# A transformer block on one core: prologue without GpSimd fills and DMA spreads, and a modelled list schedule in place of fixed alternation

## Chip, cores and metric

The kernel runs on one core of one Trainium2 chip. The metric is the device time of one execution in microseconds (us), as the median over several executions. A trace shows one execution, and its span is some 2 us shorter than the reported time. Ratios: the mean time of one kernel's runs over that of the kernel before in the same rounds. So a ratio is not quite the ratio of the medians quoted beside it.

## The reference, cut to what matters

```python
# x: (1, 2048, 512) bf16; 32 heads of 16; gated layer of width 1792
def block(x, wqkv, wo, w_gate, w_up, w_down):
    n = layernorm(x)
    q, k, v = split_heads(n @ wqkv)                      # 32 heads, Dh = 16
    p = softmax(q @ k.T * Dh ** -0.5)                    # 32 x 2048 x 2048 exponentials
    h = x + merge_heads(p @ v) @ wo
    m = layernorm(h)
    return h + (sigmoid(m @ w_gate) * (m @ w_up)) @ w_down
```

The exponentials are the bulk. There are 134 million of them, that is 2048 units of 128 x 512 (4 chunks of 512 queries, 8 groups of 4 heads, 16 key tiles, 4 heads).

## The kernel before: the parts that matter

Three units make one tile of scores, so there are 683 tiles. The matmul engine (PE) writes a tile's scores into one of two PSUM buffers of three banks, ScalarE takes the exponential, and PE multiplies it by the values ("value matmuls", into `acc`). In some tiles (here called splits) ScalarE does only two units. VectorE computes the third one in seven instructions, of which the first, J, is the one that frees the bank. All other work (projections for later heads, output projection, layernorm and gated layer of the chunk before) is "background": generators that hand out matmuls two at a time into one further PSUM bank, `pm`.

The prologue fills constant rows with memsets, some of them on GpSimd:

```python
    for g in range(2):
        nc.vector.memset(QT[g][:], 0.0)
    nc.vector.memset(KT[0][:], 1.0)
    nc.gpsimd.memset(KT[1][:], 1.0)
    nc.gpsimd.memset(Vaug[:, :, :, DH:VW], 0.5)
    # ... (layernorm, transposes, first projections: see the whole kernel)
    for g in range(2, NG):                      # no input: GpSimd starts them at once
        nc.gpsimd.memset(QT[g][:], 0.0)
        nc.gpsimd.memset(KT[g][:], 1.0)
```

The main loop alternates by a fixed rule. Even tiles get up to eight value matmuls, and odd ones get four background matmuls. VectorE's work is placed by two running clocks:

```python
        if n % 2 == 0:
            av(8)
            run_bg(0)
        else:
            tokens -= run_bg(4 if tokens >= 4 else 0)     # +1.3 tokens per tile, no cap
        run_chain(clock["A"] + 600)                       # VectorE's chain, up to 0.6 us ahead
        clock["D"] = max(clock["D"], clock["A"] - 600)
```

Of the kernel before, what the change touches and what calls it, by code (L numbers as in the profile page):

```python
# [28 lines left out]
def kernel(  # L29
# [12 lines left out]
    P = 128  # L42
# [30 lines left out]
    eps4_t = const.tile([P, 1], FP32)  # L73
    sel = const.tile([P, 32], BF16)
    xnT = [const.tile([P, DC, QC], BF16, name=f"xnT{c}") for c in range(NQC)]
# [12 lines left out]
    wv_sb = prep.tile([P, DC, D], BF16)  # L88

    wqkv_v = A_wqkv.rearrange("(c p) n -> p c n", p=P)  # L90
    x_v = A_x[0].rearrange("(t p) d -> p t d", p=P)
    for i, q in enumerate((nc.sync, nc.scalar, nc.sync, nc.scalar)):
        q.dma_start(out=xb[0][:, i, :], in_=x_v[:, i, :])
    nc.sync.dma_start(out=xb[1][:], in_=x_v[:, TQ:2 * TQ, :])
    nc.scalar.dma_start(out=wk_sb[:], in_=wqkv_v[:, :, D:2 * D])
    nc.sync.dma_start(out=xb[2][:], in_=x_v[:, 2 * TQ:3 * TQ, :])
    nc.scalar.dma_start(out=wq_sb[:], in_=wqkv_v[:, :, 0:D])
    nc.sync.dma_start(out=xb[3][:], in_=x_v[:, 3 * TQ:4 * TQ, :])
    nc.sync.dma_start(out=wv_sb[:], in_=wqkv_v[:, :, 2 * D:3 * D])

    make_identity(nc, ident_bf[:])
    nc.vector.memset(eps_t[:], 1e-5)
    nc.vector.memset(eps4_t[:], 4e-5)
    nc.gpsimd.tensor_scalar(out=ident2[:], in0=ident_bf[:], scalar1=2.0, scalar2=None, op0=ALU.mult)
    nc.vector.memset(sel[:], 0.0)
    nc.vector.tensor_reduce(out=sel[:, 0:8], in_=ident_bf[:].rearrange("p (r k) -> p r k", k=DH),
                            axis=AX.X, op=ALU.max)
    for g in range(2):
        nc.vector.memset(QT[g][:], 0.0)
    nc.vector.memset(KT[0][:], 1.0)  # L110
    nc.gpsimd.memset(KT[1][:], 1.0)
    nc.gpsimd.memset(Vaug[:, :, :, DH:VW], 0.5)
    wo_v = A_wo.rearrange("(p a j d) n -> a j d p n", a=2, j=4, d=DH)


    clock = {"D": 0.0}

    def dv(ns):
        clock["D"] += ns

    def ln_stats(src, mv):
        dv(870)
        st = small.tile([P, nc.vector.BN_STATS_DIM], FP32, name="st")
        nc.vector.bn_stats(out=st[:], in_=src)
        nc.vector.bn_aggr(out=mv, in_=st[:])
# [13 lines left out]
    def spread(dst_pair, src, cols, groups=(0, 1), queues=(nc.sync,)):  # L139
        for a in groups:  # L140
            for j in range(4):
                r = (4 * a + j) * DH
                queues[j % len(queues)].dma_start(out=dst_pair[a][32 * j:32 * j + DH, cols],  # L143
                                                  in_=src[r:r + DH, :])

    def stage(ps, name):
        dv(680)
        st = work.tile([P, QC], BF16, name=name, bufs=2)
        nc.vector.tensor_copy(out=st[:], in_=ps)
        return st  # L150

    def square(src):
        dv(430)
        sq = work.tile([P, QC], BF16, name="sq", bufs=4)
        nc.vector.tensor_tensor(out=sq[:], in0=src[:], in1=src[:], op=ALU.mult)
        return sq

    def k_fin(k4, p):
        dv(300)
        nc.vector.tensor_reduce(out=kcol[p][:], in_=k4[:], axis=AX.X, op=ALU.max)  # L160
        nc.vector.tensor_scalar(out=kcol[p][:], in0=kcol[p][:], scalar1=-0.505, scalar2=None,
                                op0=ALU.mult)

    def q_shift(ps, p):
        dv(740)
        sh = work.tile([8, QC], BF16, name="sh")
        nc.vector.tensor_scalar(out=sh[:], in0=ps[0:8, :], scalar1=-0.505,
                                scalar2=kcol[p][:, 0:1], op0=ALU.mult, op1=ALU.add)
        for a in range(2):
            nc.sync.dma_start(out=QT[2 * p + a][DH:P:32, :], in_=sh[4 * a:4 * a + 4, :])  # L170
# [6 lines left out]
    def v_out(ps, t, act):  # L177
        dst = Vaug[:, t, :, 0:DH]
        src = ps.rearrange("p (h d) -> p h d", d=DH)
        if act:  # L180
            nc.scalar.copy(out=dst, in_=src)
        else:
            dv(680)
            nc.vector.tensor_copy(out=dst, in_=src)

# [9 lines left out]
    NV0 = 6  # L195
    k4 = small.tile([8, NQC], FP32, name="k4a", bufs=1)
    mvs, rstds = {}, {}
    kps, sqs0 = {}, {}

    def c_stats(c):  # L200
        mvs[c] = small.tile([P, TQ, nc.vector.BN_AGGR_DIM], FP32, name="mv")
        for i in range(TQ):
            ln_stats(xb[c][:, i, :], mvs[c][:, i, :])
        rstds[c] = small.tile([P, TQ], FP32, name="rstd")
        nc.scalar.activation(out=rstds[c][:], in_=mvs[c][:, :, 1], func=ACT.Sqrt,
                             bias=eps_t[:, 0:1])

    def c_apply(c, dve):
        nc.vector.reciprocal(out=rstds[c][:], in_=rstds[c][:])
        for i in range(TQ):  # L210
# [4 lines left out]
            pt = transpose4(bank0(), xn)  # L215
            dst = xnT[c][:, :, i * P:(i + 1) * P]
            if i in dve:
                nc.vector.tensor_copy(out=dst, in_=pt)
            else:
                nc.scalar.copy(out=dst, in_=pt)  # L220

    def c_keys(c):
        pk = bank0()
        proj8(pk, wk_sb, 0, c)
        kd = work.tile([P, QC], BF16, name="kd", bufs=2)
        nc.scalar.copy(out=kd[:], in_=pk)
        cols = slice(c * QC, (c + 1) * QC)
        if c < NQC - 1:
            spread(KT[0:2], kd, cols)
        else:  # L230
            spread(KT[0:2], kd, cols, groups=(0,), queues=(nc.sync, nc.scalar))
        kps[c] = kd

    def c_ksq(c):
        sq = square(kps[c])
        pm = bank0()
        nc.tensor.matmul(pm[0:8, :], lhsT=sel[:, 0:8], rhs=sq[:], start=True, stop=True)
        return pm

    def c_kred(c, pm):  # L240
        nc.vector.tensor_reduce(out=k4[:, c:c + 1], in_=pm[0:8, :], axis=AX.X, op=ALU.max)

    def c_v(t):
        ps = bank0()
        v_mm(ps, t)
        v_out(ps, t, True)

    c_stats(0)
    c_stats(1)
    c_apply(0, ())  # L250
    c_stats(2)
    c_keys(0)
    c_apply(1, ())
    pq = bank0()
    proj8(pq, wq_sb, 0, 0)
    qd = work.tile([P, QC], BF16, name="qd", bufs=2)
    nc.scalar.copy(out=qd[:], in_=pq)
    spread(QT[0:2], qd, slice(0, QC))
    c_stats(3)
    c_keys(1)  # L260
    c_apply(2, (0, 2))
    pm0 = c_ksq(0)
    sqq = square(qd)
    pq = bank0()
    nc.tensor.matmul(pq[0:8, :], lhsT=sel[:, 0:8], rhs=sqq[:], start=True, stop=True)
    c_apply(3, (0, 1, 3))
    c_keys(2)
    c_kred(0, pm0)
    pm1 = c_ksq(1)
    c_kred(1, pm1)  # L270
    c_v(0)
    c_keys(3)
    pm2 = c_ksq(2)
    c_kred(2, pm2)
    c_v(1)
    nc.scalar.activation(out=small.tile([P, 1], FP32, name="warm")[:], in_=eps_t[:], func=ACT.Exp)
    pm3 = c_ksq(3)
    c_kred(3, pm3)
    k_fin(k4, 0)
    q_shift(pq, 0)  # L280
    spread(KT[0:2], kps[NQC - 1], slice((NQC - 1) * QC, S), groups=(1,))
    for t in range(2, NV0):
        c_v(t)
    for a in range(2):
        for j in range(4):
            r = 32 * j + DH * a
            nc.gpsimd.dma_start(out=wo_sb[r:r + DH, :, :], in_=wo_v[a, j])
    for g in range(2, NG):
        nc.gpsimd.memset(QT[g][:], 0.0)
        nc.gpsimd.memset(KT[g][:], 1.0)  # L290
# [14 lines left out]


    EV = "ev"

    def prep_v(t):
        yield 2  # L310
        ps = pm_tile()
        v_mm(ps, t, 0, 2)
        yield 2
        v_mm(ps, t, 2, 4)
        yield EV
        v_out(ps, t, False)

    kpend = {}

    def prep_k(p):  # L320
        sqs = []
        for c in range(NQC):
            yield 2
            ps = pm_tile()
            proj8(ps, wk_sb, p, c, 0, 2)
            yield 2
            proj8(ps, wk_sb, p, c, 2, 4)
            yield EV
            kd = stage(ps, "kd")
            spread(KT[2 * p:2 * p + 2], kd, slice(c * QC, (c + 1) * QC))  # L330
            sqs.append(square(kd))
        yield 2
# [4 lines left out]
        yield EV  # L337
        dv(680)
        kr = small.tile([P, 1], FP32, name="kr")
        nc.vector.tensor_reduce(out=kr[:], in_=ps, axis=AX.X, op=ALU.max)  # L340
        kq = small.tile([8, NQC], FP32, name="k4")
        for c in range(NQC):
            nc.sync.dma_start(out=kq[:, c:c + 1], in_=kr[32 * c:32 * c + 8, :])
        kpend[p] = kq

    def prep_q(qc, p):
        yield 2
        ps = pm_tile()
        proj8(ps, wq_sb, p, qc, 0, 2)
        yield 2  # L350
        proj8(ps, wq_sb, p, qc, 2, 4)
        yield EV
        qd = stage(ps, "qd")
        spread(QT[2 * p:2 * p + 2], qd, slice(0, QC))
        sq = square(qd)
        yield "wait"
        yield 1
        ps = pm_tile()
        nc.tensor.matmul(ps[0:8, :], lhsT=sel[:, 0:8], rhs=sq[:], start=True, stop=True)
        yield EV  # L360
        if p in kpend:
            k_fin(kpend.pop(p), p)
        q_shift(ps, p)

    OT = {}
# [3 lines left out]
    def rstd_newton(dst, var):  # L369
        n = var.shape[1]  # L370
        dv(2200)
# [3 lines left out]
        nc.vector.tensor_scalar(out=v[:], in0=var, scalar1=1e-5, scalar2=None, op0=ALU.add)  # L375
        nc.vector.tensor_scalar(out=t[:].bitcast(I32), in0=v[:].bitcast(I32), scalar1=1,
# [341 lines left out]
    while bg:  # L718
        advance()
# [89 lines left out]
```

## Time and profile before

| kernel before | us |
|---|---|
| time, median of the first 5 runs (1071.23 to 1073.19) | 1072.81 |
| median of 16 runs (these five and eleven that ran beside the kernel after) | 1069.81 |
| prologue, to the first exponential (timeline) | 53.3 |
| attention loop, to the end of the last exponential | 956.7 |
| tail (last layernorm and gated layer) | 59.4 |

From the page of the profile: the busy time of each engine, and the costliest group of instructions. A group's line has its count, busy time, mean ns of one, and the idle time before its instructions with what ended it.

```profile
span 1069.4 us, 14381 instructions
...
PE 833.8 (78%) x5124; PEld 228.4 (21%) x5188; DVE 704.3 (66%) x1670; ACT 914.0 (85%) x782; POOL 22.4 (2%) x29
...
L690 ACT ACTIVATE pt<-pss 128x1536 bf16<-128x1536 f32 (+1 forms) x683 | 868.1, 1383 | 70.9 <-PE pss L555 67.9
```

ScalarE (ACT) is the busiest engine, at 85%, nearly all of it exponentials. The groups kept apart by shape show its two kinds of exponential, full tiles and splits:

```profile
L690 ACT ACTIVATE pt<-pss 128x1536 bf16<-128x1536 f32 x508 | 712.3, 1487 | 63.0 <-PE pss L555 60.4 <-PE acc L613 0.2
...
L690 ACT ACTIVATE pt<-pss 128x1024 bf16<-128x1024 f32 x175 | 179.0, 1081 | 7.8 <-PE pss L555 7.5
```

The means of 1.487 and 1.081 us can't be read as the pace, because one exponential overlaps the end of the one before. In the timeline, the starts of consecutive ScalarE instructions have a usual distance of 1.331 us after a full exponential, 0.904 us after a split one and 0.477 us after a tanh. This document uses two numbers made from these. The **floor** of a loop is the sum of those distances over its instructions: 508 x 1.331 + 175 x 0.904 + 42 x 0.477 = 854.4 us. The **loss** is the length of the loop minus the floor. Here that is 956.7 - 854.4 = 102.3 us by which ScalarE fell behind its own pace. It stood idle for 75 us of that (it was busy for 881.3 us of the loop). Most of the rest, 23 us, belongs to the same gaps: in the trace each of the 164 gaps costs 0.12 us (median) more than its own length, because the overlap with the instruction before is lost.

The view of waits (who waited for whom; us in total, times, longest) says what for:

```profile
ACT pt L690 <- PE pss L555: 67.9, 89, 4.4
PE pss L555 <- DVE J L626: 58.2, 65, 3.0
...
PE pm L130 <- DVE hn L414: 11.1, 3, 3.8
...
PE pm L445 <- DVE hT L450: 8.2, 9, 2.3
```

ScalarE waits for scores (67.9 us). PE's scores in turn wait for J on VectorE (58.2 us), and PE's background matmuls wait for VectorE as well.

Where attention runs alone (but for 8 background matmuls in the stretch shown), the clock granted to PE is about half. The columns of this view are the stretch, its length, the busy time of each engine with its instructions, the granted clock, the DMA share and GB/s:

```profile
core 0: us, PE busy (x) PEld busy (x) DVE busy (x) ACT busy (x) POOL busy (x), PEclk, DMA share, GB/s
173.00:293.00 120.00, 95.23 (x536) 17.18 (x535) 71.94 (x177) 110.93 (x89) 0.00 (x0) 0.54 0.16 53
```

The prologue has one more thing to see. A line's view (count, shortest/median/longest ns) of VectorE's normalisation:

```profile
L212 DVE TENSOR_SCALAR xn<-xb,mv,rstd x16: 397/406/10691, 12.5 to 39.0; 128x512 bf16<-128x512 bf16 x16
```

And the timeline around the long one:

```profile
12.37 1.83 POOL L290 MEMSET KT<- 128x2048 bf16 x1
...
12.52 11.65 DVE L212 TENSOR_SCALAR xn<-xb,mv,rstd 128x512 bf16<-128x512 bf16 x4
...
21.23 1.83 POOL L290 MEMSET KT<- 128x2048 bf16 x1
...
23.26 1.25 PE L130 MATMUL b<-ident_bf,xn 128*128 128x128 bf16 x10 [23.26 <-DVE xn L212]
```

The first of the four `xn` starts at 12.52, and the four together last 11.65 us although three of them need 0.4 us each. The first of them is the long one, with 10.69 us. It ends at 23.21, just after the last GpSimd memset (21.23 + 1.83 = 23.06), and PE, which transposes `xn`, starts at 23.26.

### The profile page before, as it was taken

To read this page: it belongs to the slowest core of one execution; us is meant where nothing else is said; L and a number is where in the kernel's file an instruction comes from. 1 tells how busy PE (TensorE), PEld (TensorE's weight loads), DVE (VectorE), ACT (ScalarE), POOL (GpSimd) and SP (SyncE) were. 2 spreads that over 40 slices of the span, in tenths; PEclk is the share of its full clock that TensorE was granted. 3 is DMA by queue.
4 is the path that set the end of the run, shared out by engine and by line. 5 is a ranking of instruction groups with operands and counts; after the bars stand their busy time and mean duration, and the time that the engine had idled before them with its cause. 6 is when DMAs were issued, how large, how long until landed. Compare 5 with 4: busy or idle time off the path is not lost.

```text
span 1069.4 us, 14381 instructions
## 1 busy us (share of the span) xinstructions
PE 833.8 (78%) x5124; PEld 228.4 (21%) x5188; DVE 704.3 (66%) x1670; ACT 914.0 (85%) x782; POOL 22.4 (2%) x29
## 2 busy tenths in 40 slices
PE   0797777888787887977779888877878888778868
PEld 0322111111122222211112222211122222211133
DVE  8577555556666776675677777765577667756441
ACT  1498778998998999999989999989989999999732
POOL 8000000000000000000000000000000000000000
PEclk9998786555577999976588999966589999955589
DMA  6000001500000000000000000000000000000000
GB/s 157 23 3 20 23 21 55 186 1 6 1 16 1 1 1 6 11 26 6 1 16 1 1 1 6 19 20 24 1 16 1 1 1 11 11 1 1 1 0 20
DMA packets 20135, 19.16 MB, mean 18 GB/s; under 512 B 5216, under 2 KB 18912, under 8 KB 20064
## 3 DMA queue, kind: packets, MB, share of 16 engines
q1 hardware_dynamic: 18400, 16.37, 5.2%
q10 hardware_dynamic: 1408, 1.34, 0.4%
q8 instruction: 41, 0.67, 0.3%
q0 software_dynamic: 256, 0.52, 0.2%
q14 instruction: 30, 0.25, 0.1%
HBM read 11.80 MB, written 2.10 MB: 13 GB/s over the span
## 4 chain that ended last, share of the span: by engine, by line
ACT 33%; DVE 24%; PE 24%; issue 15%; SPq 2%; DMA 1%; ACTq 0%; DVEq 0%
ACT pt L690 32%; PE pss L555 9%; DVE J L626 6%; PE acc L613 5%; PE pm L445 3%; DVE dr L646 2%; DVE dq L644 2%; PE pm L136 2%; DVE db L642 2%; SPq L143 2%; DVE da L635 1%; DVE hT L450 1%; PE gu L445 1%; PE hp L774 1%; DVE xs L576 1%
## 5 line engine op out<-in xcount | busy, mean ns | idle before, releaser
L690 ACT ACTIVATE pt<-pss 128x1536 bf16<-128x1536 f32 (+1 forms) x683 | 868.1, 1383 | 70.9 <-PE pss L555 67.9
L555 PE MATMUL pss<-QT,KT 32*128 32x512 bf16 x2048 | 325.8, 470 | 152.1 <-ACT pt L690 85.9
L613 PE MATMUL acc<-pt,Vaug 128*17 128x512 bf16 x1874 | 287.9, 478 | 0.1
L626 DVE TENSOR_SCALAR J<-pss 128x512 uint16<-128x512 f32 x174 | 119.3, 685 | 188.7 <-PE pss L555 188.7
L555 PEld LDWEIGHTS <-KT 32*128 32x128 bf16 x2048 | 85.0, 94 | 499.1 <-issue 375.6
L646 DVE SCALAR_TENSOR_TENSOR dr<-J,dq 128x512 uint16<-128x512 uint16 x174 | 120.2, 691 | 5.5
L644 DVE TENSOR_TENSOR dq<-dq,db 128x512 bf16<-128x512 bf16 x174 | 73.7, 424 | 5.3
L613 PE MATMUL acc<-dr,Vaug 128*17 128x512 bf16 x174 | 74.6, 465 | 0.5 <-DVE dr L646 0.5
L613 PEld LDWEIGHTS <-Vaug 128*17 128x17 bf16 x2048 | 47.5, 91 | 127.7 <-issue 119.9
L642 DVE TENSOR_TENSOR db<-da,db 128x512 bf16<-128x512 uint16 x174 | 72.5, 417 | 0.0
L445 PE MATMUL pm<-xnT,wg 128*128 128x512 bf16 x185 | 51.3, 391 | 11.1 <-DVE hT L450 8.2
L635 DVE TENSOR_SCALAR da<-J 128x512 uint16<-128x512 uint16 x174 | 50.6, 291 | 4.4
L639 DVE TENSOR_SCALAR dq<-da 128x512 bf16<-128x512 uint16 x174 | 49.7, 285 | 0.0
L637 DVE TENSOR_SCALAR db<-J 128x512 uint16<-128x512 uint16 x174 | 49.6, 285 | 0.0
L450 DVE SCALAR_TENSOR_TENSOR hT<-th,pm 128x512 bf16<-128x512 f32 x42 | 28.6, 681 | 27.1 <-PE pm L445 22.4
L455 PE MATMUL pm<-wd,hT 128*128 128x512 bf16 x154 | 43.9, 388 | 3.1 <-DVE ob L461 2.5
L445 PE MATMUL pm<-xnT,wu 128*128 128x512 bf16 x155 | 43.5, 393 | 2.4
L468 ACT ACTIVATE th<-pm 128x512 f32<-128x512 f32 x49 | 32.5, 664 | 14.5 <-PE pm L445 14.5
L576 DVE STREAM_TRANSPOSE xs<-acc 128x512 f32<-128x512 f32 x32 | 22.8, 713 | 24.5 <-PE acc L613 24.3
L445 PEld LDWEIGHTS <-wg 128*128 128x128 bf16 x224 | 20.3, 100 | 38.5 <-issue 22.4
L130 PE MATMUL b<-ident_bf,xn 128*128 128x128 bf16 x64 | 7.1, 278 | 27.0 <-DVE xn L212 27.0
L445 PEld LDWEIGHTS <-wu 128*128 128x128 bf16 x224 | 20.6, 99 | 29.6 <-issue 12.6
(115 smaller groups left out, 426.8 us busy)
## 6 DMA issues: line engine op xcount, KB each, us to landing
QT<-qd SPq DMA_DIRECT2D x128, 16.0 KB
out_dram<-ob SPq DMA_DIRECT2D x16, 128.0 KB
KT<-kd SPq DMA_DIRECT2D x126, 16.0 KB
wg<-in_B_w_gate_dram SPq DMA_DIRECT2D x1, 1792.0 KB
wu<-in_B_w_up_dram SPq DMA_DIRECT2D x1, 1792.0 KB
wd<-in_B_w_down_dram SPq DMA_DIRECT2D x1, 1792.0 KB
xb<-in_A_x_dram SPq DMA_DIRECT2D x3, 512.0 KB
xr<-in_A_x_dram SPq DMA_DIRECT2D x12, 128.0 KB
```

What stands on the lines that cost most here:

```text
L445: nc.tensor.matmul(ps, lhsT=w[:, d, f * P:(f + 1) * P], rhs=hnT[:, d, :], start=(d == 0), stop=(d == DC - 1))
L455: nc.tensor.matmul(ps, lhsT=hT[:, f, i * P:(i + 1) * P], rhs=wd[:, f, :], start=(f == 0), stop=(f == FC - 1))
L555: mm = nc.tensor.matmul(pss[:, ui, :], lhsT=KT[g][32 * j:32 * j + 32, kt * P:(kt + 1) * P], rhs=QT[g][32 * j:32 * j + 32, :], start=True, ...
L613: nc.tensor.matmul(acc[32 * j:32 * j + VW, :], lhsT=Vaug[:, kt, 4 * g + j, :], rhs=un.ap, start=(c == 0), stop=(c == NT - 1), tile_positio ...
L626: first = nc.vector.tensor_scalar(out=J[:], in0=src, scalar1=512 * SC * LOG2E, scalar2=512 * 127.0, op0=ALU.mult, op1=ALU.add)
L635: (210, lambda: V.tensor_scalar(out=a[:], in0=J[:], scalar1=511, scalar2=None, op0=ALU.bitwise_and)),
L637: (210, lambda: V.tensor_scalar(out=b[:], in0=J[:], scalar1=0xFE00, scalar2=None, op0=ALU.bitwise_or)),
L639: (250, lambda: V.tensor_scalar(out=q[:], in0=a[:], scalar1=EXP_C1 / (512 * 512 * 4), scalar2=EXP_C0 / (512 * 4), op0=ALU.mult, op1=ALU.add)),
L642: (400, lambda: V.tensor_tensor(out=b[:].bitcast(BF16), in0=a[:], in1=b[:].bitcast(I16), op=ALU.mult)),
L644: (450, lambda: V.tensor_tensor(out=q[:], in0=q[:], in1=b[:].bitcast(BF16), op=ALU.mult)),
L646: (680, lambda: V.scalar_tensor_tensor(out=r[:], in0=J[:], scalar=0.25, in1=q[:], op0=ALU.mult, op1=ALU.add)),
L690: ex = nc.scalar.activation(out=pt[:, 0:wa, :], in_=pss[:, 0:wa, :], func=ACT.Exp, scale=SC)
```

## The change

The intent is to start the first exponential earlier and to keep ScalarE fed in the loop. Core of the diff, with cuts marked:

```diff
 # prologue: fills and first projections
-    nc.gpsimd.memset(KT[1][:], 1.0)
+    for g in range(1, NG):
         nc.vector.memset(QT[g][:], 0.0)
+    def ones_fill(g):                                  # a DMA from a tile of ones
+        nc.sync.dma_start(out=KT[g][:]..., in_=ones[:]...to_broadcast([P, NQC, QC]))
-    for g in range(2, NG):
-        nc.gpsimd.memset(QT[g][:], 0.0)
-        nc.gpsimd.memset(KT[g][:], 1.0)
-    NV0 = 6                                            # value tiles projected before the loop
+    NV0 = 16
+    # K and Q of group 0 from weights padded to 32 columns a head: they land in place,
+    # no DMA spread; two of the first layernorm statistics on ScalarE ...

 # loop: jobs with modelled ends
+    T = {"P": 0.0, "A": 0.0, "D": 0.0}                 # modelled time of PE, ScalarE, VectorE
+    # VectorE/ScalarE work waits in dq/aq as Job(ns, fn, deps) and is placed when deps end
+    def try_bg(tokens, loose=60.0):
+        ns, mm, deps = bg[0][2]
+        r = max(ends of deps) + LAT
+        if tokens < mm or r > T["P"] + loose:          # not ready in the model: don't issue
+            return 0
-        if n % 2 == 0:
-            av(8)
-            run_bg(0)
-        else:
-            tokens -= run_bg(4 if tokens >= 4 else 0)
-        run_chain(clock["A"] + 600)
+        tokens = min(tokens + (3.0 if n < 24 else 2.0 if n < 72 else 1.35), 8.0)
+        hor = max(T["A"], sc_end.get(n + 1, 0.0) + LAT)
+        lim = ex_end[n] + LAT                          # when the next scores may be written
+        while T["P"] < lim - 150:                      # fill PE only up to there
+            run_dve(min(T["P"], hor))
+            ready = len(av_ready(60.0))
+            if (ready >= 6 or 0 < ready == left()) and av(8):
+                continue
+            used = try_bg(tokens)
+            if used:
+                tokens -= used
+                continue
+            if (ready >= 3 or 0 < ready == left()) and av(8):
+                continue
+            T["P"] += 100
+        run_dve(hor)

 # tail: layernorm statistics, rsqrt and apply per 128 rows instead of in one block;
 # one down-projection of the chunk before is held back to run there
 # ... (the rest of the diff moves existing operations into such jobs)
```

## The prediction

> **What bounds the kernel now.** Three stages, read from the timeline: prologue 0 to 53.3 us (first exponential), attention loop to 1010 us, tail 59 us.
>
> Loop: ScalarE's exponentials set the pace. The groups view has 508 of width 1536 and 175 of width 1024 (in those VectorE computes the third 512 columns). Back to back they start 1.331 and 0.904 us apart in the timeline; with 42 tanh at 0.48 us that is a floor of 854 us, and the loop takes 957. So about 103 us is ScalarE not fed. By stretches of 42 tiles the loss is 11.6 and 12.1 us (K/Q/V projections squeezed in), 6 to 7 with attention alone, 7 to 9 around the output projection and layernorm, only 2 to 3 in the gated stage. The waits view agrees: scores wait for the previous exponential (86 us) and for VectorE's J (58 us), ScalarE for scores (68 us). The windows view shows a granted clock of 0.53 to 0.59 where attention runs alone and 0.9 to 1.0 where dense projections are mixed in. The Trainium skill (TensorE: Matmul & The Clock Gate, Part 1) says the clock has two states, released by recent activity; this trace agrees: its clock records hold only 0.5 and 1.0.
>
> Prologue: one VectorE xn takes 10.69 us where its siblings take 0.40, ending when GpSimd's memsets of KT/QT end. The Trainium skill (SBUF — State Buffer, Who interferes with whom) says GpSimd and two-port VectorE operations lock one port pair exclusively; the trace fits.
>
> **What the change does.**
> 1. Prologue: the KT fills become DMAs, QT fills go to VectorE; K0/Q0 use padded weights, so no DMA spread precedes the first score. Removes the 10.3 us block and about 4 us of DMA; adds memsets and ten more V tiles (40 matmuls, about 9 us at 0.22 us). First exponential at about 43 us instead of 53: minus 10.
> 2. Loop: a list schedule with modelled PE/ACT/DVE times replaces fixed alternation. Background matmuls come at up to 3, 2, then 1.35 per tile, tokens capped at 8, so the gated stage spreads over most of a chunk instead of finishing early. I expect the clock to stay near 1.0 from the second chunk on and the attention-alone loss to shrink there; the first chunk's second half stays cold (0.5). Splits rise slightly, 174 to about 200: one costs VectorE 2.75 us exclusively, is barred in the last quarter of each group, and saves ScalarE 0.427 us, so minus 11 us. Loss falls from 103 to about 50 us: 7 in the projections, 14 in the cold part, 28 elsewhere. Loop about 895 us: minus 62.
> 3. Tail: layernorm pipelined per tile, one held down-projection warms PE: minus 4.
>
> Sum: 1073 - 10 - 62 - 4, rounded up for new waits: **1000 us, 80% range 970 to 1032**. Chances: faster 0.94, same 0.05, slower 0.01.
>
> **What would show it.** First exponential between 39 and 47 us; no xn above 1 us. Splits 180 to 225. ScalarE busy share of the span above 88% (85 now). Clock mean about 0.9 (0.80 now); cold stretch only in tiles 60 to 171. Waits of scores for J and of ScalarE for scores halved. First gate matmul of the last stage under 16 us after the last exponential (17.5 now).
>
> **What would make it wrong.** The schedule models warm matmul times; where PE is cold, six-matmul attention batches (1.03 against 0.60 us) overrun and ScalarE starves, as before. If 1.35 matmuls per tile don't hold the clock up, or a background queue is too slow and is forced at a group's start, the loop stays above 930. More splits than 225, or losses under 3%, would take it below 970.

## More of the kernel before

A background step whose evacuation is on VectorE asks only that a later tile has begun (`EV`), not when VectorE will be through.

One such wait, in the timeline of the chunk boundary (start, us, engine, line, operation, and in brackets the idle time before it):

```profile
320.98 0.39 PE L555 MATMUL pss<-QT,KT 32*128 32x512 bf16 x3
...
324.19 0.16 DVE L385 TENSOR_TENSOR rstd<-ny,nt 128x4 f32<-128x4 f32 x1
324.39 0.55 DVE L414 TENSOR_SCALAR hn<-h,mv,rstd 128x512 bf16<-128x512 f32 x1
...
325.00 0.45 PE L130 MATMUL pm<-ident_bf,hn 128*128 128x128 bf16 x4 [3.62 <-DVE hn L414]
...
325.38 0.61 PE L555 MATMUL pss<-QT,KT 32*128 32x512 bf16 x3
...
326.09 4.29 ACT L690 ACTIVATE pt<-pss 128x1536 bf16<-128x1536 f32 x3 [2.48 <-PE pss L555]
```

PE stood 3.62 us in front of a transpose of `hn`, which VectorE had not written yet. The next scores come after it in PE's program, so they came late and ScalarE idled 2.48 us. The Trainium skill (TensorE: Matmul & The Clock Gate, Part 2) says that matmuls stay in program order, and this stretch agrees: the scores start only at 325.38, behind the transposes.

## The result

| | before | after |
|---|---|---|
| time, median (range, runs), us | 1069.81 (1064.44 to 1073.19, 16) | 985.23 (980.80 to 987.21, 9) |
| ratio, 95% interval | 1 | 0.9205 (0.9184 to 0.9226) |
| first exponential, us | 53.3 | 42.6 |
| loop, us: floor + loss | 956.7: 854.4 + 102.3 | 883.3: 845.0 + 38.3 |
| loss in tiles 0 to 60, 60 to 171, the rest | 15.6, 21.4, 65.3 | 8.6, 6.9, 22.8 |
| tail, us | 59.4 | 56.8 |
| splits | 174 | 196 |
| mean granted clock | 0.799 | 0.896 |

The page after, in the same places:

```profile
span 982.7 us, 14502 instructions
...
PE 808.6 (82%) x5137; PEld 236.7 (24%) x5213; DVE 739.2 (75%) x1842; ACT 902.7 (92%) x804; POOL 2.9 (0%) x7
...
L841 ACT ACTIVATE pt<-pss 128x1536 bf16<-128x1536 f32 (+1 forms) x683 | 850.0, 1426 | 22.5 <-PE pss L686 16.6
```

ScalarE is now at 92% of a span that is 87 us shorter. The groups by shape, with 22 exponentials more of the short kind:

```profile
L841 ACT ACTIVATE pt<-pss 128x1536 bf16<-128x1536 f32 x486 | 696.4, 1544 | 17.6 <-PE pss L686 12.0 <-PE acc L754 4.5 <-ACT pt L841 0.5
...
L841 ACT ACTIVATE pt<-pss 128x1024 bf16<-128x1024 f32 x197 | 223.0, 1135 | 4.8 <-PE pss L686 4.6
```

The waits that answer to those before:

```profile
ACT pt L841 <- PE pss L686: 16.6, 31, 1.5
...
PE pss L686 <- DVE J L774: 10.5, 22, 1.2
...
PE pm L579 <- DVE hT L583: 3.4, 9, 0.6
```

The scores' wait for J fell from 58.2 to 10.5 us, and ScalarE's for scores from 67.9 to 16.6. The same place at the chunk boundary in the timeline after:

```profile
297.26 0.41 DVE L572 COPY xnT<-pm 128x512 bf16<-128x512 bf16 x1
...
297.59 0.54 DVE L565 TENSOR_SCALAR hn<-h,mv,rstd 128x512 bf16<-128x512 f32 x1
297.72 0.59 PE L161 MATMUL pm<-ident_bf,hn 128*128 128x128 bf16 x4 [0.26 <-DVE xnT L572]
...
298.24 0.61 PE L686 MATMUL pss<-QT,KT 32*128 32x512 bf16 x3
298.35 0.42 DVE L572 COPY xnT<-pm 128x512 bf16<-128x512 bf16 x1 [0.22 <-PE pm L161]
...
299.23 1.45 ACT L841 ACTIVATE pt<-pss 128x1536 bf16<-128x1536 f32 x1 [0.20 <-ACT pt L841]
```

No transpose of `hn` in this stretch waits for `hn`. The one wait, 0.26 us, is for VectorE's copy that frees the bank `pm`. The code puts transposes into PE's program only where the schedule expects `hn` to be there. The normalisation of the prologue, and the start of the loop:

```profile
L218 DVE TENSOR_SCALAR xn<-xb,mv,rstd x16: 404/406/414, 8.9 to 25.2; 128x512 bf16<-128x512 bf16 x16
```

```profile
29.94 12.25 PE L178 MATMUL b<-wv_sb,xnT 128*128 128x512 bf16 x55
...
42.12 0.60 PE L686 MATMUL pss<-QT,KT 32*128 32x512 bf16 x6
...
42.58 4.62 ACT L841 ACTIVATE pt<-pss 128x1024 bf16<-128x1024 f32 x4 [0.63 <-PE pss L686]
```

No `xn` is long, and the first exponential starts at 42.58. PE spends the 12.25 us before it on the value projections that moved in front of the loop. The stretch of the first chunk in which attention runs alone (here with 16 background matmuls, of 591) is no longer at half clock, but not at full clock either:

```profile
163.00:283.00 120.00, 97.76 (x591) 24.08 (x590) 91.59 (x231) 116.05 (x96) 0.00 (x0) 0.73 0.03 6
```

So of the 86.7 us between the two spans, 10.8 came from the prologue, 73.3 from the loop (9.4 of floor and 64.0 of loss) and 2.6 from the tail.

### The profile page after: what moved, and what is told of

Same layout as the page of the kernel before. It is cut to its first block, busy times and chain, and to the rows that moved or that the text cites. A ratio compares the mean times of both kernels' runs of the same rounds, so it can differ in the third digit from the quotient of the medians.

```text
span 982.7 us, 14502 instructions
## 1 busy us (share of the span) xinstructions
PE 808.6 (82%) x5137; PEld 236.7 (24%) x5213; DVE 739.2 (75%) x1842; ACT 902.7 (92%) x804; POOL 2.9 (0%) x7
## 4 chain that ended last, share of the span: by engine, by line
ACT 37%; PE 21%; DVE 19%; issue 18%; SPq 3%; DMA 2%; ACTq 0%; DVEq 0%
ACT pt L841 34%; PE pss L686 6%; PE acc L754 4%; DVE J L774 3%; DVE dr L794 3%; PE pm L579 2%; DVE dq L792 2%; PE pm L167 2%; SPq L174 2%; DVE db L790 2%; ACT th L599 1%; PE gu L579 1%; DVE hT L583 1%; PE b L178 1%; PE hp L967 1%
## 5 line engine op out<-in xcount | busy, mean ns | idle before, releaser
L841 ACT ACTIVATE pt<-pss 128x1536 bf16<-128x1536 f32 (+1 forms) x683 | 850.0, 1426 | 22.5 <-PE pss L686 16.6
L686 PE MATMUL pss<-QT,KT 32*128 32x512 bf16 x2048 | 296.3, 423 | 123.7 <-ACT pt L841 101.7
L754 PE MATMUL acc<-pt,Vaug 128*17 128x512 bf16 x1852 | 297.9, 424 | 2.3 <-ACT pt L841 0.6
L686 PEld LDWEIGHTS <-KT 32*128 32x128 bf16 x2048 | 92.7, 92 | 395.6 <-issue 291.3
L774 DVE TENSOR_SCALAR J<-pss 128x512 uint16<-128x512 f32 x196 | 133.6, 682 | 66.1 <-PE pss L686 65.9
L794 DVE SCALAR_TENSOR_TENSOR dr<-J,dq 128x512 uint16<-128x512 uint16 x196 | 134.8, 688 | 4.7
L754 PEld LDWEIGHTS <-Vaug 128*17 128x17 bf16 x2048 | 59.2, 88 | 174.1 <-issue 170.2
L792 DVE TENSOR_TENSOR dq<-dq,db 128x512 bf16<-128x512 bf16 x196 | 83.0, 424 | 6.1
L790 DVE TENSOR_TENSOR db<-da,db 128x512 bf16<-128x512 uint16 x196 | 81.6, 416 | 0.0
L783 DVE TENSOR_SCALAR da<-J 128x512 uint16<-128x512 uint16 x196 | 56.8, 290 | 4.3
L583 DVE SCALAR_TENSOR_TENSOR hT<-th,pm 128x512 bf16<-128x512 f32 x42 | 28.7, 683 | 30.0 <-PE pm L579 25.9
L728 DVE STREAM_TRANSPOSE xs<-acc 128x512 f32<-128x512 f32 x32 | 22.8, 711 | 9.8 <-PE acc L754 9.5
L593 DVE SCALAR_TENSOR_TENSOR ob<-pm,h 128x512 bf16<-128x512 f32 x12 | 8.3, 689 | 27.5 <-PE pm L588 27.4
```

Of the source, the lines that this page charges most:

```text
L686: mm = nc.tensor.matmul(pss[:, ui, :], lhsT=KT[g][32 * j:32 * j + 32, kt * P:(kt + 1) * P], rhs=QT[g][32 * j:32 * j + 32, :], start=True, ...
L754: nc.tensor.matmul(acc[32 * j:32 * j + VW, :], lhsT=Vaug[:, kt, 4 * g + j, :], rhs=un.ap, start=(c == 0), stop=(c == NT - 1), tile_positio ...
L774: first = nc.vector.tensor_scalar(out=J[:], in0=src, scalar1=512 * SC * LOG2E, scalar2=512 * 127.0, op0=ALU.mult, op1=ALU.add)
L783: (215, lambda: V.tensor_scalar(out=a[:], in0=J[:], scalar1=511, scalar2=None, op0=ALU.bitwise_and)),
L790: (440, lambda: V.tensor_tensor(out=b[:].bitcast(BF16), in0=a[:], in1=b[:].bitcast(I16), op=ALU.mult)),
L792: (450, lambda: V.tensor_tensor(out=q[:], in0=q[:], in1=b[:].bitcast(BF16), op=ALU.mult)),
```

## Experiments

Twelve kernels ran in three sets of three rounds each, always beside the kernel before. All gave correct results. The kernel after did not run again in these sets, so its variants are compared with it through their ratios to the kernel before. This table collects them. Floor and loss are worked out from each one's trace as above.

| run | ratio (95%) | splits | floor | loss |
|---|---|---|---|---|
| before | 1 | 174 | 854.4 | 102.3 |
| before, no GpSimd fills | 0.9922 (0.9888 to 0.9957) | 174 | 854.4 | 101.5 |
| before, filler matmuls | 0.9876 (0.9844 to 0.9908) | 174 | 854.4 | 88.3 |
| before, VectorE held back | 0.9813 (0.9789 to 0.9837) | 174 | 854.4 | 82.7 |
| before, these three together | 0.9636 (0.9603 to 0.9669) | 174 | 854.4 | 72.6 |
| before, fine alternation | 1.0415 (1.0385 to 1.0444) | 172 | 855.2 | 148.7 |
| after | 0.9205 (0.9184 to 0.9226) | 196 | 845.0 | 38.3 |
| after, background early | 0.9230 (0.9202 to 0.9257) | 193 | 846.3 | 38.7 |
| after, filler matmuls | 0.9225 (0.9191 to 0.9258) | 195 | 845.4 | 42.7 |
| after, VectorE far ahead | 0.9232 (0.9184 to 0.9280) | 200 | 843.3 | 39.6 |
| after, blind background | 0.9347 (0.9327 to 0.9368) | 200 | 843.3 | 53.7 |
| after, coarse alternation | 0.9444 (0.9414 to 0.9473) | 202 | 842.4 | 64.3 |
| after, six value tiles in front | 0.9262 (0.9227 to 0.9297) | 196 | 845.0 | 54.4 |
| after, 173 splits | 0.9334 (0.9305 to 0.9363) | 173 | 854.8 | 43.4 |

The prediction's explanation of the loop was theory C: the background is spread, so PE's clock stays up and ScalarE is fed. The rivals are about the order of instructions.

### l1_before_filler: is it the clock? (in the kernel before)

```diff
             tokens -= run_bg(4 if tokens >= 4 else 0)
+            if not bg and n + 4 < len(tiles):
+                ps = pm_tile()
+                for i in range(4):
+                    nc.tensor.matmul(ps, lhsT=wq_sb[:, i, 0:P], rhs=xnT[2][:, i, :],
+                                     start=(i == 0), stop=(i == 3))
```

> The kernel before, plus four dense matmuls of 128x128 by 128x512 into the background bank on every second tile while the background queue is empty (488 in all), results never read. Theory C (the low clock is what starves ScalarE where attention runs alone): the granted clock rises from 0.80 to about 0.95, the stretches with attention alone lose 3% in place of 10%, and the kernel gets 20 to 30 us faster although it does 488 matmuls more. Rival O (the order of instructions starves it, whatever the clock): the clock rises but the time stays within 8 us of before, or grows by the PE time of the filler.

Measured: 1054.60 us, ratio 0.9876. The same stretch as before, with filler:

```profile
173.00:293.00 120.00, 103.58 (x708) 31.09 (x719) 72.56 (x178) 114.00 (x92) 0.00 (x0) 0.96 0.16 53
```

Useless work made the kernel about 13 us faster. The clock rose from 0.54 to 0.96 in this stretch, and the loss in tiles 84 to 168 fell from 13.2 to 5.8 us. That is more than rival O allowed (8) and less than theory C asked (20). The low clock was a real cost in the kernel before, but a minor one.

### l2_after_fast_bg and l3_after_filler: is it the clock? (in the kernel after)

```diff
-        tokens = min(tokens + (3.0 if n < 24 else 2.0 if n < 72 else 1.35), 8.0)
+        tokens = min(tokens + (3.0 if n < 24 else 2.0), 8.0)
```

> The kernel after, with 2.0 tokens per tile from tile 72 on in place of 1.35, so that the background of a chunk is through early, as before, and attention runs alone for the last third of a chunk. Theory C: mean clock falls from 0.90 to about 0.82 and the time grows by 8 to 15 us. Rival O: the clock falls and the time stays within 4 us of after's 0.9205 of before, since the order is unchanged in kind.

```diff
                 tokens -= used
                 continue
+            if not bg and tokens >= 2 and n + 4 < N:
+                ps = pm_tile()
+                for i in range(2):
+                    nc.tensor.matmul(ps, lhsT=wq_sb[:, i, 0:P], rhs=xnT[2][:, i, :], ...)
+                T["P"] += 2 * MM
+                tokens -= 2
+                continue
```

> The kernel after, plus two dense matmuls whenever the background queue is empty and a token pair is there (190 in all), never read. Theory C: the clock rises from 0.90 to about 0.97; ScalarE's loss at low clock (26 us of 38 in the trace of after) falls by 8 to 15 us, ratio to before about 0.909. Rival O: no gain, ratio 0.918 to 0.925.

Measured: 986.04 and 986.16 us, ratios 0.9230 and 0.9225. Both intervals overlap that of after. The mean clock was 0.955 with filler. With the background early it fell from 0.896 to 0.849:

```profile
core 0: 984.4 us, clock 0.849
```

So between mean clocks of 0.849 and 0.955 the new schedule takes the same time, and theory C falls as the main reason for the gain. It is not nothing, though. With filler, the loss in tiles 84 to 168 did fall, from 5.2 to 1.6 us, but it rose elsewhere. Part of that rise, in tiles 0 to 42 (6.3 to 8.7 us), lies before the first filler at tile 71, so single traces differ by 2 or 3 us in such a stretch. Another part the filler made itself, because this edit doesn't ask whether `pm` is free. Its first matmul at tile 71, and the exponential that came late after it:

```profile
143.48 0.59 PE L870 MATMUL pm<-xnT,wq_sb 128*128 128x512 bf16 x1 [3.01 <-DVE sh L488]
...
146.21 1.45 ACT L841 ACTIVATE pt<-pss 128x1536 bf16<-128x1536 f32 x1 [3.81 <-PE pss L686]
```

The same happens at tile 505 (ScalarE idle for 3.46 us). Without these two waits, some 7 us, the filler would have gained about 3 us of loss, by estimate from 42.7 - 38.3 - 7.3. That is still under the 8 us that theory C asked for.

The stretch of tiles 84 to 168 lets clock and order be read side by side. In the old order the loss there was 13.2 us at a clock of 0.53, and 5.8 with filler at 0.98. In the new order it was 5.2 at 0.71, and 1.6 with filler at 1.00. So both count there. How much of the fall from 13.2 to 5.2 came by way of the clock, which rose from 0.53 to 0.71, is not separated: l2 left the clock of this stretch at 0.70.

### l4_after_dve_ahead and l6_before_dve_held: is it J standing late?

```diff
 # l4, kernel after
-        run_dve(hor)
+        run_dve(hor + 1000.0)
 # l6, kernel before
-        run_chain(clock["A"] + 600)
+        run_chain(clock["A"] - 400)
```

> The kernel after, with VectorE's queue filled 1 us past the arrival of the next scores (so the next J, which frees the score bank, stands behind other VectorE work, as before); 200 splits in place of 196. Theory J (not letting J stand late is a main part of the gain): waits of the scores for J rise from 10.5 us to 50 or more, ScalarE loses 20 to 35 us more, ratio about 0.945. Rival (VectorE's order is not what mattered): ratio stays within 0.5% of 0.9205.

> The kernel before, with VectorE's spare chain queued no further ahead than at the first of its two calls per tile (0.4 us short of the end of the exponential, in place of 0.6 us past it); 174 splits still. Theory J in the form left after the run with VectorE ahead (a queue laid too far ahead delays J and the evacuations that PE waits for): waits of scores for J fall from 58 us to under 35 and the time by 10 to 25 us, ratio 0.975 to 0.99. Rival: nothing changes, ratio 0.995 to 1.005.

Measured for l4: 984.53 us, ratio 0.9232. Waits of scores for J rose only to 17.3 us, not to 50. The rival held. Measured for l6: 1048.72 us, ratio 0.9813, some 20 us less by one changed number, with as many splits as before. The line of the waits of l6, to be read against 58.2 us before:

```profile
PE pss L555 <- DVE J L626: 12.8, 9, 3.0
```

Letting VectorE run 0.6 us past the exponential put J behind other work and cost the kernel before about 20 us. It is J, and not the evacuations, that gained: PE's waits of background for VectorE did not fall (for `hn` 11.1 before and 12.7 here). That the new schedule bears VectorE far ahead is measured. Its model counts the end of J among what the next scores wait for, and gives PE other work until then. That this is the reason is read from the code and not shown.

### g2_before_fine and g1_after_alternate: is it the size of the blocks in front of the scores?

Between two groups of scores, PE's program before has mostly blocks of 5 to 8 value matmuls or 4 dense ones. After, it has mostly 3 value matmuls, or 3 and 2 dense ones. Each was given the pattern of the other:

```diff
 # g2, kernel before
-        if n % 2 == 0:
-            av(8)
-            run_bg(0)
-        else:
-            tokens -= run_bg(4 if tokens >= 4 else 0)
+        av(4)
+        tokens -= run_bg(2 if tokens >= 2 else 0)
 # g1, kernel after
-            if (ready >= 6 or 0 < ready == left()) and av(8):
+            if n % 2 == 0 and (ready >= 6 or 0 < ready == left()) and av(8):
-            used = try_bg(tokens)
+            used = try_bg(tokens) if n % 2 else 0
-            if (ready >= 3 or 0 < ready == left()) and av(8):
+            if n % 2 == 0 and (ready >= 3 or 0 < ready == left()) and av(8):
```

> The kernel before, with up to four value matmuls and up to two background matmuls on every tile, in place of eight and four on alternate ones; 172 splits. Theory G: the loss of 102 us falls by 30 us or more, ratio 0.97 or less. Rival D: the loss stays or grows, as background still waits in PE's queue for VectorE; ratio 0.985 to 1.02.

> The kernel after, but value matmuls only on even tiles and background only on odd ones, as before: between two groups of scores the program of PE then has blocks of 6 to 8 value matmuls or 2 to 4 dense ones, in place of 3 and 3+2. 202 splits. Theory G (the size of the blocks that stand in front of the scores in PE's queue is the main part of the loop's gain): ScalarE's loss rises from 38 us to 70 or more, ratio to before 0.95 or more. Rival D (issuing background only when what it reads is there, and not the block size): ratio stays within 0.5% of 0.9205.

Measured for g2: 1113.07 us, ratio 1.0415, slower by 44 us. Theory G falls here outright, and rival D had not expected more than 1.02 either. The waits of g2 show part of the reason:

```profile
ACT pt L690 <- PE pss L555: 111.1, 141, 5.8
...
PE pm L445 <- DVE hT L450: 25.9, 32, 2.3
...
PE pm L445 <- ACT th L468: 14.0, 35, 0.7
```

PE's wait of gate matmuls for VectorE rose from 8.2 to 25.9 us, and the waits for ScalarE's tanh (14.0) are not among the listed ones of before. With background on every tile, each step stands in PE's queue right behind the evacuation that it needs, and the fixed rule doesn't look.

Measured for g1: 1009.49 us, ratio 0.9444, between the two expectations. The loss is 26 us more than after's, and it does not lie where block size would put it. Five single waits of over 2 us make up 31.8 us of it (after has two such, 4.6 us together). In nine of the 16 stretches of 42 tiles the loss is within 0.2 us of after's or below it. Four of the five waits lie where a group or chunk begins (after tiles 20, 41, 340 and 511), and the waits view has four waits of scores for the DMA of query rows, 21.3 us together. The one after tile 340, in the timeline:

```profile
496.25 0.37 PE L686 MATMUL pss<-QT,KT 32*128 32x512 bf16 x1 [0.64 <-ACT pt L841]
...
502.36 0.61 PE L686 MATMUL pss<-QT,KT 32*128 32x512 bf16 x2 [5.73 <-DMA QT<-sh]
...
503.07 1.02 ACT L841 ACTIVATE pt<-pss 128x1024 bf16<-128x1024 f32 x1 [5.52 <-PE pss L686]
```

The first scores of a new chunk waited 5.73 us for the DMA that brings its query rows. The background that makes them had fallen behind and was forced at the boundary. So coarse blocks cost mainly where background misses its deadline. In steady running they cost little.

### g3_after_blind_bg: is it issuing by readiness?

```diff
-        if tokens < mm or r > T["P"] + loose:
+        if tokens < mm:
             return 0
-        T["P"] = max(T["P"], r) + ns
+        T["P"] += ns
```

> The kernel after, with background matmuls put into PE's queue whether or not the modelled time of what they wait for has come (the wait itself stays, in PE). 200 splits. Theory D: PE stands in waits of background matmuls for VectorE, ScalarE's loss rises by 15 us or more, ratio 0.935 or more. Theory G: within 0.5% of 0.9205.

Measured: 998.87 us, ratio 0.9347, about 14 us slower than after, with 4 splits more. Theory D expected this size:

```profile
PE pm L579 <- ACT th L599: 16.7, 17, 1.4
...
PE pm L579 <- DVE hT L583: 5.6, 13, 0.8
```

The first of these two waits is not among after's listed ones at all, and the second was 3.4 us. Issuing by readiness is a cause, of some 15 us of loss. (The edit also stops the model from adding such waits to PE's time. What each of the two is worth was not tried.)

### p1_before_no_pool_fills: what held the prologue?

```diff
+    ones = const.tile([P, QC], BF16, name="ones")
+    nc.vector.memset(ones[:], 1.0)
+    for g in range(2, NG):
+        nc.vector.memset(QT[g][:], 0.0)
     for g in range(2, NG):
-        nc.gpsimd.memset(QT[g][:], 0.0)
-        nc.gpsimd.memset(KT[g][:], 1.0)
+        nc.sync.dma_start(out=KT[g][:]..., in_=ones[:]...to_broadcast([P, NQC, QC]))
```

> The kernel before with the GpSimd fills of KT and QT of groups 2 to 7 gone: KT filled by DMA from a tile of ones, QT by VectorE at the start. Theory L (the 10.69 us of one xn is VectorE locked out by GpSimd's memsets, and all of it lies on the critical path): no xn above 1 us, first exponential at about 43 us in place of 53, time 9 to 11 us less, ratio about 0.990. Rival (the xn waits for something else, such as its data): the xn stays long, ratio 0.998 to 1.002.

Measured: 1060.54 us, ratio 0.9922, first exponential at 43.25 us.

```profile
L216 DVE TENSOR_SCALAR xn<-xb,mv,rstd x16: 402/406/414, 12.9 to 29.2; 128x512 bf16<-128x512 bf16 x16
```

The long `xn` is gone, the first exponential moved by 10.1 us, and the loop is as long as before (955.9 us). Theory L is shown as far as the memsets go: they held the `xn`, and all of it was on the critical path. By what means they held it, no run tests. The rest of the prologue's rewrite is worth less than 1 us in the time to the first exponential (43.25 against 42.58), although it fits ten more value projections into that time. With six value tiles, as here, it is worth 9.0 us (34.25 in the next run, p3).

### p3_after_six_v: do the value projections belong in front of the loop?

```diff
-    NV0 = 16
+    NV0 = 6
-    queue(prep_k(0, (1,)), ("k", 0))
+    for t in range(NV0, NT):
+        queue(prep_v(t), ("v", t))
+    queue(prep_k(0, (1,)), ("k", 0))
```

> The kernel after with 6 value projections in the prologue in place of 16; the other ten are first in the background queue, as before. Theory V (moving them out is part of the loop's gain, since the first tiles have no room for them): first exponential 8 to 9 us earlier (about 34 us), but the loss of the first 84 tiles rises by 10 us or more, so the time is equal or worse: ratio 0.919 to 0.930. Rival (they fit into the loop for nothing): 5 us or more faster than after, ratio 0.916 or less.

Measured: 989.84 us, ratio 0.9262. The first exponential came at 34.25, which is 8.3 us earlier. The loss of the first 42 tiles rose from 6.3 to 24.4 us, nearly all of it in one wait (the last number is the longest):

```profile
ACT pt L839 <- PE pss L686: 33.5, 32, 20.3
```

At the start of the second group, K and Q of that group were not made yet. Moving the projections in front pays because of that deadline. The run queues the ten value tiles ahead of K and Q of the second group, though. Leaving them in the loop behind K and Q was not tried.

### l5_after_fewer_splits: what is a split worth?

```diff
-        split = (len(tl) == GU and
+        split = (len(live_all) * N < 174 * (n + 1) and len(tl) == GU and
```

> The kernel after with the number of tiles whose last third VectorE computes held down to 173, as before, in place of 196. The sum of the prediction: each costs ScalarE 0.427 us, so the floor rises by 23 x 0.427 = 9.8 us and the time by 7 to 11 us, ratio 0.927 to 0.932. Rival (VectorE is the scarcer one and fewer splits relieve it): less than 3 us, ratio under 0.9235.

Measured: 998.55 us, ratio 0.9334, some 14 us slower than after, which is more than expected. The floor rose by 9.8 us exactly as reckoned, and the loss by 5.1 us on top. The 22 further splits are thus a cause of the gain. Why the loss grew too stays open.

### c1_before_three: do the causes add up?

The kernel before with the edits of p1, l6 and l1 together.

> The kernel before with three of the edits together: no GpSimd fills, VectorE's chain held back (alone 0.9813), filler matmuls while the background queue is empty (alone 0.9876). If the three causes are separate, their savings add: 10 + 20 + 13 = 43 us, ratio about 0.960. If the filler and the held chain cure the same stalls, less: 0.967 to 0.975. What is left to after's 0.9205 is then due to splits, the value projections' place and the issue of background by readiness.

Measured: 1030.31 us, ratio 0.9636. The three single savings, 0.78%, 1.87% and 1.24%, add to 3.89%, that is 0.9611. This lies inside the interval. Within the noise they act as separate causes, and together they make up about 39 of the 85 us. By ratio, no version tried beats the kernel after.

## Why the prediction was right

The measured 985 us lies in the range of 970 to 1032 and is 15 us under the central value. Point by point:

- **Prologue, minus 10.** Measured minus 10.8. The mechanism is shown by the run without GpSimd fills.
- **Splits, 174 to about 200, minus 11 us.** Measured 196, and 9.4 us of floor. The run with 173 splits returned 9.8 us of floor and 5.1 of loss.
- **Loss in the loop, 103 to about 50.** Measured 38.3. This is the term that was mis-sized. Of its three parts, "7 in the projections" was 8.6 (tiles 0 to 60), "14 in the cold part" was 6.9 (tiles 60 to 171), and "28 elsewhere" was 22.8. The two last explain 12 of the 15 us by which the prediction was high.
- **Why the loss would fall.** Here the reasoning failed though the sum held. The prediction said "I expect the clock to stay near 1.0 from the second chunk on and the attention-alone loss to shrink there". The clock did rise, to 0.896 as forecast, and filler that warms it saves 13 us in the kernel before. But in the kernel after, lowering it to 0.849 or raising it to 0.955 left the time the same within the noise (the filler that raised it made some 7 us of waits of its own, so a gain of a few us is not excluded). What the runs show in its place are J no longer standing behind other VectorE work (20 us in the kernel before), background issued when its inputs are there (14 us in the kernel after), and background that meets the start of the next group or chunk (16 us of loss more when the value projections are moved back, 26 when the loop's order is made coarse).
- **"The first chunk's second half stays cold (0.5)".** Wrong. It ran at 0.74 on average over tiles 60 to 171. Why the new order keeps the clock higher there, with 24 background matmuls in place of 31, is not settled.
- **"Six-matmul attention batches (1.03 against 0.60 us) overrun and ScalarE starves".** Not the main thing. The run with coarse alternation has such batches and lost most of its time in four waits at the start of a group or chunk. In tiles 84 to 168, at a clock of 0.64, it lost 7.8 us against 5.2.
- **Tail, minus 4.** Measured minus 2.6. The first gate matmul came 14.4 us after the last exponential (17.5 before), inside the 16 that was named. No run took the tail apart.
- **Named signs.** First exponential 39 to 47 (42.6), no `xn` above 1 us (0.41), splits 180 to 225 (196), ScalarE above 88% (92), and both waits halved (10.5 and 16.6) all came out. One did not: "cold stretch only in tiles 60 to 171". The windows of the kernel after have 0.84 in 643 to 763 us too.

Not settled: the remaining 34 us of loss between the three edits together (72.6) and the kernel after (38.3). The runs on the after side that touch it (15.4 us for blind background, 26.0 for coarse alternation, 16.1 for the value projections) were each measured alone. They were not measured together, so how much they overlap is unknown.

## What to carry to other kernels

When one engine sets the pace, sum the usual start-to-start distances of its instructions and compare that floor with the time taken: the difference, and not busy shares, says what a schedule can win. In an engine that works in order, an instruction queued before its inputs exist delays the urgent one behind it, so place background work by when its inputs will be there and when its result is due; a finer fixed rhythm alone made this kernel 4% slower. Before crediting a gain to a clock that rose along with it, move the clock both ways, for which a few matmuls that nobody reads are enough.

## What the Trainium skill lacked or had wrong

- SBUF — State Buffer, Who interferes with whom: the exclusive lock between GpSimd and two-port VectorE operations agrees with the trace. It says that the operation that starts first keeps the ports for the whole instruction, and not what follows when one side has a queue of them: a 0.41 us `xn` was held for 10.3 us, across nine GpSimd memsets back to back, and got in after the last. The kernel after has what looks like a small second case, in its timeline: a VectorE operation on 4 columns lasts 1.25 us and ends as GpSimd's memset does (3.53 and 3.50).

```profile
1.24 2.26 POOL L110 MEMSET Vaug<- 128x512 bf16 x1
...
2.28 1.25 DVE L120 TENSOR_SCALAR selq<-sel 128x4 bf16<-128x4 bf16 x1
```

- TensorE: Matmul & The Clock Gate, Part 1: the two clock states agree (all clock records are 0.5 or 1.0). The page ties the state to how busy PE is, and doesn't say how matmuls that use part of the array count. In the kernel before, PE was busy 95 of 120 us, nearly all of it with 32-row and 17-column matmuls, and the granted clock was 0.54. With four dense matmuls added on every second tile, PE was busy 104 us and the clock was 0.96.
- No page has it: the attention-alone stretch of the kernel after, with the same kinds of matmuls in another order, ran at 0.73 (98 of 120 us busy). Tiles 84 to 168 have the same number of background matmuls in both kernels (8), and took 115.6 us at a clock of 0.53 before and 105.9 us at 0.71 after. What makes the difference isn't settled by these runs.
